# The last step of a spectral branch: block transposes on VectorE replaced by DMAs inside SBUF, and its final matmuls in 64x64 tiles

## The chip, the core and the metric

The kernel runs on one core of one Trainium2 chip. The metric is the device time of one execution in microseconds (us), lower being better. The kernel before takes 149.45 us (median of three runs, 148.86 to 152.55).

## The reference

The kernel computes a gated mix of two branches over the same input x of 2048 positions and 512 channels, in fp32:

```
g = sigmoid((x * gate_w).sum(-1))                # one gate per position
a = irfft2(rfft2(x) * (w_r + 1j * w_i))          # branch A: a 2-D spectral filter
b = irfft(rfft(x, 2L) * rfft(K, 2L))[:L] + x * D_skip   # branch B: a long convolution along positions
out = g * a + (1 - g) * b
```

K is the kernel of a state space model, made from log_A_real, A_imag, C_real, C_imag and log_dt. With the inputs given, every channel of B falls under a test that allows a running sum over positions (a scan) in place of the convolution. A counter of such channels is read at the end; a general path behind it is in the program and isn't taken.

## The kernel before

Branch A is a mixed-radix transform. A position is split as 32 x 64; the kernel works on 32 *slots* (frequencies of the short transform) and handles the slots in nine units: eight pairs and a half one. A hand-written order, the string PLAN, names the work word by word: a letter is a function, a digit its unit. Each word's instructions go to their engines in this order, and each engine runs its own queue in order; all loads, stores and copies that SP issues stand in one queue.

The words, with the lines of the profile of before:

- `f`/`F`, `C`, `c` (L228 to L240): fold the input, first matmuls, a DVE block transpose into AR.
- `P`, `t`, `D`, `d`, `Z`, `z`, `y` (L351 to L390): transform along positions and along channels for one unit, with PE, ACT and DVE taking turns in PSUM.
- `W`, `U` (L403, L405) on DVE, `p`, `g` (L412 to L425) on GpSimd, `h` (L431): the product with the weights w.
- `I`, `i`, `V` (L440 to L453): back along channels; `V` writes the result of a unit into AI, two pieces of 128 x 256 or more for each unit.
- `B`, `e` (L478 to L485): first step back along positions, p_ia, copied from PSUM into AI by ACT. The words `v`, `w`, `j`, `K`, `E`, `H` do the same for one unit in halves of its channels (L496, L499).
- `b` (L503): eight DVE block transposes in place over the whole of AI (seen as VA, 32 columns of 256 channels), which put the slots on the partitions for the last step.
- `Y`, `s` (L511, L516): branch B. PE transposes the scanned x (XT) four columns at a time, ACT scales the result by 1 - g into AR.
- `Q` (L528): the last step of A: for each of 32 columns, one matmul of a 128x128 matrix s1a by VA's 256 columns into p_oa.
- `q` (L549, DVE) or `a`, `A` (L539 on ACT, L543 on GpSimd): g times the result is added to AR, and two stores of 256 KB go out for each group of four columns.

XT is built by `X`, `x`, `m`, `o`, `r`, `k` (L273 to L292): a scan on DVE, and an accumulating DMA (XT<-v, issued by GpSimd) or a DVE instruction (L292) that adds it to the scaled x.

Most intermediate tiles come from one pool, "blk", of 13 blocks; the next tile waits until the oldest one's readers are done. Eight semaphores serve SP's DMAs in turn, so a ninth DMA waits for the first of the eight.

Of the kernel before, what the change touches and what calls it, by code (L numbers as in the profile page):

```python
# [26 lines left out]
ALU = mybir.AluOpType  # L27
# [12 lines left out]
F1 f0 C0 c0 C1 R2 f2 R5 R3 f3 l2 c1 F4 C2 c2 f5 C4 N0 F6 X0 l3 R4 C5 R1 c4 C6 f8 C8 N1 N2 G4 F9 R0 c5 l0 X1 l1 c8 c6  # L40
C9 C3 c9 f7 N3 x0 X2 C7 c3 R6 c7 P1 P0 J0 G5 x1 t1 J1 t0 D1 m0 m1 J2 x2 m2 P2 P4 L2 L1 D0 R9 d1 z1 Z1 y1 t2 D2 t4 W1
U1 L3 d0 z0 p1 Z0 L0 y0 W0 l4 d2 z2 Z2 y2 U0 P6 P5 U2 R8 g1 P3 t5 t6 D5 W2 R7 L4 p0 g0 t3 X3 x3 l5 h1 D3 z3 m3 d3 d5
l7 L5 Z3 z5 y3 h0 W3 U3 l6 p2 I1 i1 V1 G0 P7 g2 Z5 o3 p3 o0 L6 y5 G1 G2 t7 W5 D4 d4 I0 g3 U5 p5 g5 h3 D6 z4 Z4 S3 D7
i0 V0 y4 U4 o1 L7 W4 d7 z6 G3 d6 Z6 h5 l8 y6 z7 r0 P8 p4 t8 B1 W6 Z7 e1 y7 h2 U6 g4 I5 i5 o2 p6 D8 z8 L8 W7 g6 U7 p7
d8 h4 V5 I3 r1 i3 V3 x4 o4 I2 i2 B3 e3 I4 Z8 y8 m4 g7 h6 i4 V2 x6 W8 h7 I6 i6 U8 V6 V4 I7 S2 p8 i7 V7 m6 k6 g8 h8 B2
B6 e6 e2 I8 i8 v8 B5 x7 S1 e5 B4 x5 m7 j8 e4 w8 E8 o5 K8 H8 S0 B7 e7 m5 r2 k7 Y4 Y7 Y1 Y6 b1 s7 s4 Y3 s3 Y0 s0 Y2 Y5
b6 s6 s1 b2 b3 b0 b4 s5 b5 b7 Q6 s2 Q0 q6 q0 Q5 q5 Q3 q3 Q7 Q4 q4 a7 Q2 A7 q2 Q1 q1
# [5 lines left out]
PARTS = [slice(a, b) for a, b in zip([0, 8, 16, 32, 48, 64, 80, 96, 112, 120], [8, 16, 32, 48, 64, 80, 96, 112, 120, 128])]  # L53
CHANNELS = np.concatenate([_T, 256 + _T, 511 - _T, 255 - _T])


def _consts():
# [54 lines left out]
    s2p = s2p.transpose(1, 0, 2)  # L112
# [9 lines left out]
    s1b = np.zeros((32, 2, 2, 32, 32, 2))  # L122
    s1a = np.zeros((32, 2, 2, 16, 2, 2, 32, 2))
    for g in range(2):
        s1b[:, g, :, :, :, g] = s1i[32 * g:32 * g + 32]
        for e in range(2):
            for dh in range(2):
                s1a[:, g, :, :, e, dh, :, g] = s1i[32 * g:32 * g + 32, :, :16] * 2 / 512 * (-1) ** (e * dh)
    s1b = s1b.reshape(32, 128, 64).transpose(1, 0, 2)
    s1a = s1a.reshape(32, 128, 128).transpose(1, 0, 2)  # L130
# [23 lines left out]
def body(ctx: ExitStack, tc: tile.TileContext, x, xg, xt, w, wh, prms, vecs, gw, dskip,  # L154
# [14 lines left out]

    AI = keep.tile([P, 17, D], F32, name="AI")  # L170
    VA = AI[:, 0:16].rearrange("p s (e d) -> p (s e) d", e=2)
# [7 lines left out]
    X = AI.rearrange("p s d -> p (s d)")[:, 0:8192]  # L179

    last = AI[:, 16]
# [11 lines left out]
    gws = work.tile([P, 4, 32], F32, name="gws")  # L193

# [8 lines left out]
    with tc.manual_schedule():  # L203
# [90 lines left out]

        def G_(k):
# [152 lines left out]
        def V_(u, ks=(0, 1)):  # L448
            pr = UNITS[u]
            n = nrow(pr) // 64  # L450
            ai = AI[:, 2 * pr:2 * pr + n].rearrange("p s (h k t) -> p s h k t", h=2, k=2)
            for k in ks:
                V.tensor_tensor(ai[:, :, :, k], t_["pi", u][:, :n, :, 0], t_["po", u][:, :n], op=ALU.subtract if k else ALU.add)  # L453


        def M_(u):
            p = t_["pi", u] = psum("p_v").rearrange("p u (h n) -> p u h n", h=2)
            for v in range(nrow(UNITS[u]) // 64):
                for h in range(2):
                    a = [t_["gt", u][:, o, v, 2 * h:2 * h + 2].rearrange("p c k -> p (c k)") for o in range(2)]  # L460
                    T.matmul(p[:, v, h], a[0], dbw[:, h, 0:1].broadcast_to([P, 2, P]), start=True, stop=False)
                    T.matmul(p[:, v, h], a[1], dbw[:, h, 1:3], start=False, stop=True)

        def o_a(u, ks=slice(0, 2)):
            pr = UNITS[u]
            n = nrow(pr) // 64
            ai = AI[:, 2 * pr:2 * pr + n].rearrange("p s (h k t) -> p s h k t", h=2, k=2)
            pi = t_["pi", u][:, :n].rearrange("p s h (k t) -> p s h k t", k=2)
            S.copy(ai[:, :, :, ks], pi[:, :, :, ks])


        def B_(u):
            pr = UNITS[u]
            p = t_["pb", u] = psum("p_ia")
            for v in range(2):
                sl = 2 * pr + v
                if sl == 0:
                    T.matmul(p[:, v], s2e[:, 0], AI[:, 0], start=True, stop=False)  # L478
                    T.matmul(p[:, v], s2e[:, 16], AI[:, 16], start=False, stop=True)
                else:  # L480
                    T.matmul(p[:, v], s2p, AI[:, sl], start=True, stop=True)  # L481

        def e_a(u):
            pr = UNITS[u]
            S.copy(AI[:, 2 * pr:2 * pr + 2], t_["pb", u])  # L485


        def half(u, k):
            pr = UNITS[u]
            return AI[:, 2 * pr:2 * pr + 2].rearrange("p s (h k t) -> p k s h t", h=2, k=2)[:, k]  # L490

        def B2_(u, k):
            if k == 0:
                t_["pb", u] = psum("p_ia").rearrange("p k (s h t) -> p k s h t", s=2, h=2)
            for v in range(2):
                T.matmul(t_["pb", u][:, k, v], s2p, half(u, k)[:, v], start=True, stop=True)  # L496

        def e2_a(u, k):
            S.copy(half(u, k), t_["pb", u][:, k])  # L499

        def b_a(c):
            v = VA[:, :, 32 * c:32 * c + 32].rearrange("p b d -> p d b")
            V.transpose(v, v)  # L503


        def Y_(j):
            p = t_["py", j] = psum("p_y").rearrange("p k (b i d) -> p (k b) i d", b=2, i=2)
            xv = XT.rearrange("p (i e) (c b) -> p i (e c) b", i=2, b=32)
            for k in range(4):
                for i in range(2):  # L510
                    T.transpose(p[:, k, i], xv[:, i, :, 4 * j + k], eye)  # L511

        def s_a(j):
            for k in range(4):
                b = 4 * j + k
                S.activation(AR[:, b].rearrange("p (i d) -> p i d", i=2), t_["py", j][:, k], AF.Copy, scale=g1[:, 1, b:b + 1])  # L516
# [4 lines left out]
        def load_a(k):  # L521
            s1a[k] = work.tile([P, 8, P], F32, tag="w", name="s1a", bufs=4)
            nc.sync.dma_start(s1a[k], c_s1a[:, 8 * k:8 * k + 8])

        def Q_(j):
            p = t_["pq", j] = psum("p_oa").rearrange("p k (b d) -> p (k b) d", b=2)
            for k in range(4):
                T.matmul(p[:, k], s1a[j // 2][:, 4 * j % 8 + k], VA[:, 4 * j + k], start=True, stop=True)  # L528
# [6 lines left out]
        def a_a(j):  # L535
            t_["qs", j] = blk([P, 4, 256], "qs")
            for k in range(4):
                b = 4 * j + k
# [7 lines left out]
        def q_a(j):  # L546
            for k in range(4):
                b = 4 * j + k
                V.scalar_tensor_tensor(AR[:, b], t_["pq", j][:, k], g1[:, 0, b:b + 1], AR[:, b], op0=ALU.mult, op1=ALU.add)  # L549
# [19 lines left out]
            "v": lambda u: V_(u, (0,)), "w": lambda u: V_(u, (1,)), "j": lambda u: B2_(u, 0), "K": lambda u: B2_(u, 1), "E": lambda u: e2_a(u, 0), "H": lambda u: e2_a(u, 1),  # L569
# [225 lines left out]
```

## Time and profile before

| | us |
|---|---|
| median of three runs | 149.45 (148.86 to 152.55) |
| the profiled execution | 148.65 |
| its span | 146.8 |
| TensorE's mean granted clock in it | 0.95 of full speed |
| PE busy | 112.6 |
| DVE busy | 113.8 |
| ACT busy | 70.5 |
| GpSimd busy | 57.4 |

The profile is of one execution. The span reaches from its first to its last instruction, and the execution's time lies 1.85 us above it. PE is TensorE's matmuls, PEld its weight loads, DVE is VectorE, ACT ScalarE, POOL GpSimd, SP the engine that issues most DMAs; SPq is SP's queue. L503 is line 503 of the kernel. In a group of instructions, "out<-in" names the tiles, then come the shape, the count, the time busy, the mean of one in ns, and after the bar the time that the engine idled just before them with what ended it. An fp32 matmul is recorded as two instructions of half the work each, so 32 matmuls are 64 records.

### The profile page before, as it was taken

The page shows a single profiled execution, that of the slowest core. Times are in us where ns is not written, and L with a number is a line of the kernel's source. Part 1 is how long each engine was busy: PE and PEld are TensorE (multiplying, and loading weights), DVE is VectorE, ACT ScalarE, POOL GpSimd, SP SyncE. Part 2 cuts the span into 40 slices and gives each one's busy share as a digit, 9 for nine tenths or more (in the row PEclk, how much of TensorE's full clock was granted, in tenths as well). Part 3 has the DMA queues.
Part 4 walks back from the last instruction along what each step waited for, and adds up shares of the span by engine and source line. Part 5 has one row for each costly group of instructions (what it writes and reads, how often), then busy time and mean ns, then how long its engine had stood idle before and what let it go on. Part 6 is the DMA issues. An engine that isn't in the chain of part 4 may idle for free.

```text
span 146.8 us, 1834 instructions
## 1 busy us (share of the span) xinstructions
PE 112.6 (77%) x611; PEld 86.1 (59%) x611; DVE 113.8 (78%) x134; ACT 70.5 (48%) x136; POOL 57.4 (39%) x57
## 2 busy tenths in 40 slices
PE   7936976399989998959888878997805975999600
PEld 7811352098978982858378577462405964888400
DVE  0369999995788597759798995979689997695900
ACT  0003000337375969496789765398610699504000
POOL 0306850100059993976999979200200000003300
PEclk9999999959999999999999999999975899999985
DMA  4999999992105870404793898000191000158690
GB/s 114 318 275 418 391 417 387 413 416 99 37 7 173 287 292 0 143 5 146 132 225 91 273 214 210 4 0 0 40 214 36 0 0 0 57 205 318 223 354 19
DMA packets 9427, 25.52 MB, mean 174 GB/s; under 512 B 1568, under 2 KB 2624, under 8 KB 8512
## 3 DMA queue, kind: packets, MB, share of 16 engines
q1 hardware_dynamic: 8976, 22.16, 42.2%
q0 software_dynamic: 432, 3.15, 10.9%
q8 instruction: 7, 0.11, 0.3%
q14 instruction: 12, 0.10, 0.2%
HBM read 17.93 MB, written 4.19 MB: 151 GB/s over the span
## 4 chain that ended last, share of the span: by engine, by line
DVE 31%; PE 30%; ACT 17%; DMA 9%; issue 5%; POOL 2%; SPq 1%; DVEq 0%; ACTq 0%; POOLq 0%
DVE AR L240 9%; PE p_oa L528 8%; PE p_d L365 6%; ACT AR L516 6%; PE p_t L351 5%; DMA XT<-v 5%; PE p_v L440 5%; DMA AI<-in_x_dram 5%; DVE v L283 3%; DVE p_d L378 3%; DVE p_d L379 3%; DVE tw L405 3%; PE p_ia L481 2%; PE p_y L511 2%; DVE AR L549 2%
## 5 line engine op out<-in xcount | busy, mean ns | idle before, releaser
L351 PEld LDWEIGHTS p_t<-s2e,AR 128*128 128x128 f32 x136 | 17.4, 208 | 5.5 <-DVE AR L240 3.5
L351 PE MATMUL p_t<-s2e,AR 128*128 128x128 f32 x136 | 18.0, 294 | 3.4 <-DVE AR L240 2.7
L440 PEld LDWEIGHTS p_v<-dbw,gt 128*128 128x128 f32 x136 | 16.0, 192 | 7.5 <-issue 4.6
L440 PE MATMUL p_v<-dbw,gt 128*128 128x128 f32 x136 | 16.8, 278 | 4.6 <-ACT gs L303 1.5
L236 PE MATMUL p_s<-f,AI 128*128 128x512 f32 (+1 forms) x40 | 15.7, 527 | 5.5 <-DVE f L228 3.4
L412 POOL TENSOR_TENSOR px<-tw 128x512 f32<-128x512 f32 (+1 forms) x9 | 10.9, 1215 | 19.6 <-DVE tw L405 19.5
L503 DVE STREAM_TRANSPOSE AI<-AI 128x1024 f32<-128x1024 f32 x8 | 16.9, 2202 | 1.8 <-ACT AI L485 1.8
L365 PE MATMUL p_d<-et,dfw 128*128 128x256 f32 (+1 forms) x72 | 16.1, 371 | 0.7 <-ACT et L356 0.6
L240 DVE STREAM_TRANSPOSE AR<-p_s 128x1024 f32<-128x1024 f32 (+1 forms) x10 | 14.8, 1555 | 1.6 <-PE p_s L236 1.6
L516 ACT ACTIVATE AR<-p_y,g 128x256 f32<-128x256 f32 x32 | 11.8, 587 | 8.1 <-PE p_y L511 8.1
L528 PE MATMUL p_oa<-AI,s1a 128*128 128x256 f32 x64 | 14.1, 380 | 1.7 <-ACT AR L516 1.7
L511 PE MATMUL p_y<-eye,XT 128*128 128x128 f32 x64 | 10.0, 317 | 6.5 <-DMA XT<-v 5.6
L277 ACT ACTIVATE p_x<-XT,pers 128x1024 f32<-128x1024 f32 x8 | 9.0, 1121 | 12.5 <-POOL pers L261 10.4
L549 DVE SCALAR_TENSOR_TENSOR AR<-p_oa,g,AR 128x256 f32<-128x256 f32 x28 | 11.6, 477 | 4.2 <-PE p_oa L528 4.0
L236 PEld LDWEIGHTS p_s<-f,AI 128*128 128x128 f32 x40 | 7.1, 196 | 13.1 <-issue 4.3
L365 PEld LDWEIGHTS p_d<-et,dfw 128*128 128x128 f32 x72 | 12.7, 190 | 2.5 <-ACT et L356 1.2
L528 PEld LDWEIGHTS p_oa<-AI,s1a 128*128 128x128 f32 x64 | 12.1, 190 | 3.5 <-ACT AR L516 1.9
L543 POOL TENSOR_TENSOR AR<-AR,qs 128x1024 f32<-128x1024 f32 x1 | 2.3, 2348 | 29.2 <-ACT qs L539 29.2
L511 PEld LDWEIGHTS p_y<-eye,XT 128*128 128x128 f32 x64 | 9.2, 201 | 7.8 <-issue 6.3
L453 DVE TENSOR_TENSOR AI<-p_v,po 128x512 f32<-128x512 f32 (+1 forms) x18 | 10.9, 650 | 2.3 <-ACT po L445 2.3
L405 DVE TENSOR_TENSOR tw<-p_d,w 128x1024 f32<-128x1024 f32 x8 | 9.8, 1219 | 3.6 <-ACT p_d L390 3.6
L481 PE MATMUL p_ia<-AI,s2p 128*128 128x512 f32 x26 | 12.0, 595 | 0.0
(66 smaller groups left out, 180.6 us busy)
## 6 DMA issues: line engine op xcount, KB each, us to landing
w<-in_w_dram SPq DMA_DIRECT2D x8, 512.0 KB, 5.6
XT<-in_xt_dram SPq DMA_DIRECT2D x4, 1024.0 KB, 7.0
out_dram<-AR SPq DMA_DIRECT2D x16, 256.0 KB, 3.7
AI<-in_x_dram SPq DMA_DIRECT2D x6, 512.0 KB, 7.6
XT<-v POOLq DMA_DIRECT2D x3, 1024.0 KB, 7.0
s1a<-in_c_s1a_dram SPq DMA_DIRECT2D x4, 512.0 KB, 3.9
AI<-in_x_dram SPq DMA_DIRECT2D x4, 256.0 KB
prm<-in_prms_dram SPq DMA_DIRECT2D x3, 256.0 KB
```

The costliest lines, as they stand in the source:

```text
L236: T.matmul(p[:, u, :n], s1e, t_["f", q][:, u, :n], start=True, stop=True)
L240: V.transpose(AR.rearrange("p s (u d) -> p u d s", u=2)[:, :, PARTS[q]], t_["c", q][:, :, :32 * n].rearrange("p u (b d) -> p u d b", d=n))
L351: T.matmul(p[:, q, :, 64 * v:64 * v + 64], AR[:, 16 * (q // 2) + sl, 128 * (q % 2):128 * (q % 2) + 128], s2e[:, k], start=True, stop=True)
L365: T.matmul(p[:, o, :, h, :n], dfw[:, 2 * h + o], et[:, ::-1] if h else et, start=True, stop=True)
L405: E.tensor_tensor(t.rearrange("p o r a k -> p (o r a k)"), z.rearrange("p o q k -> p (o q k)"), w.rearrange("p o r a k -> p (o r a k)"), o ...
L440: T.matmul(p[:, v, h, o], t_["gt", u][:, o, v, 2 * h:2 * h + 2].rearrange("p c k -> p (c k)"), dbw[:, h, o], start=True, stop=True)
L481: T.matmul(p[:, v], s2p, AI[:, sl], start=True, stop=True)
L503: V.transpose(v, v)
L511: T.transpose(p[:, k, i], xv[:, i, :, 4 * j + k], eye)
L516: S.activation(AR[:, b].rearrange("p (i d) -> p i d", i=2), t_["py", j][:, k], AF.Copy, scale=g1[:, 1, b:b + 1])
L528: T.matmul(p[:, k], s1a[j // 2][:, 4 * j % 8 + k], VA[:, 4 * j + k], start=True, stop=True)
L549: V.scalar_tensor_tensor(AR[:, b], t_["pq", j][:, k], g1[:, 0, b:b + 1], AR[:, b], op0=ALU.mult, op1=ALU.add)
```

## The change

1. The eight DVE block transposes are gone. Word `b` now belongs to a unit: ACT copies p_ia into a block tile ei, and four DMAs on SP's queue (one for each slot and half of the channels) write it into VA so that the slots come to lie on the partitions. Each of the 32 DMAs reads 128 partitions of 1 KB and writes 4 partitions, 32 apart, of 32 KB. AI is gone; the input X, which shared its space, now shares VA's. `V` writes into a block tile ai, and the halves (`v`, `w`, `j`, `K`, `E`, `H`) are gone.
2. The last step `Q` is done in 64x64 tiles: for each column two matmuls, one for each half of VA's partitions, at the array's four quadrants in turn: columns k = 0 and 1 of a group of four on the diagonal, 2 and 3 on the other two. s1a holds 64 columns in place of 128 for each position.
3. The output's rows come in another order (g, half, a), so B's part must match: `s` scales into a block tile sc, and a new word `w` moves it into AR with four DMAs of 128 KB (32 partitions of 4 KB to 32 partitions). The gates go through a tile gh, and eight DMAs of 4 KB put them in the same order. The host puts the rows back.
4. PLAN is a new order. The copies `e` and DMAs `b` of the first pairs stand in the middle of the kernel; part of `Y` and `s` stands ahead of the last pairs; all of `Q` is at the end.

The general path, which isn't taken, is changed to match. The core of the diff:

```diff
-    AI = keep.tile([P, 17, D], F32, name="AI")
-    VA = AI[:, 0:16].rearrange("p s (e d) -> p (s e) d", e=2)
+    VA = keep.tile([P, 32, 256], F32, name="VA")
...
+LAST = np.array([2 * j + k % 2 + 16 * (k // 2) for j in range(8) for k in range(4)])
...
+        def regroup(dst, src):
+            for g in range(2):
+                for e in range(2):
+                    nc.sync.dma_start(dst[64 * g + 32 * e:64 * g + 32 * e + 32], src[64 * e + g:64 * e + 64:2])
...
         def V_(u, ks=(0, 1)):
             pr = UNITS[u]
             n = nrow(pr) // 64
-            ai = AI[:, 2 * pr:2 * pr + n].rearrange("p s (h k t) -> p s h k t", h=2, k=2)
+            if 0 in ks:
+                t_["ai", pr] = blk([P, 2, D], "ai")
+            ai = t_["ai", pr][:, :n].rearrange("p s (h k t) -> p s h k t", h=2, k=2)
...
         def e_a(u):
-            pr = UNITS[u]
-            S.copy(AI[:, 2 * pr:2 * pr + 2], t_["pb", u])
+            t_["ei", u] = blk([P, 2, D], "ei")
+            S.copy(t_["ei", u], t_["pb", u])
...
-        def b_a(c):
-            v = VA[:, :, 32 * c:32 * c + 32].rearrange("p b d -> p d b")
-            V.transpose(v, v)
+        def b_a(u):
+            for v in range(2):
+                for e in range(2):
+                    nc.sync.dma_start(VA[4 * UNITS[u] + 2 * v + e::32], t_["ei", u][:, v, 256 * e:256 * e + 256])
...
         def s_a(j):
+            t = t_["sc", j] = blk([P, 4, 2, P], "sc")
             for k in range(4):
-                b = 4 * j + k
-                S.activation(AR[:, b].rearrange("p (i d) -> p i d", i=2), t_["py", j][:, k], AF.Copy, scale=g1[:, 1, b:b + 1])
+                b = LAST[4 * j + k]
+                S.activation(t[:, k], t_["py", j][:, k], AF.Copy, scale=gh[:, b:b + 1])
+
+        def r_a(j):
+            regroup(AR[:, 4 * j:4 * j + 4].rearrange("p k d -> p (k d)"), t_["sc", j].rearrange("p k i d -> p (k i d)"))
...
         def load_a(k):
-            s1a[k] = work.tile([P, 8, P], F32, tag="w", name="s1a", bufs=4)
-            nc.sync.dma_start(s1a[k], c_s1a[:, 8 * k:8 * k + 8])
+            s1a[k] = work.tile([P, 16, 64], F32, tag="w", name="s1a", bufs=4)
+            nc.sync.dma_start(s1a[k], c_s1a[:, 16 * k:16 * k + 16])
 
         def Q_(j):
             p = t_["pq", j] = psum("p_oa").rearrange("p k (b d) -> p (k b) d", b=2)
-            for k in range(4):
-                T.matmul(p[:, k], s1a[j // 2][:, 4 * j % 8 + k], VA[:, 4 * j + k], start=True, stop=True)
+            for k in (0, 2, 1, 3):
+                for r in (0, 64):
+                    o = r ^ 64 * (k // 2)
+                    T.matmul(p[o:o + 64, k], s1a[j // 4][r:r + 64, 4 * (j % 4) + k], VA[r:r + 64, LAST[4 * j + k]], start=True, stop=True, tile_position=(r, o))
```

The end of the new order, from the first inner DMAs on (b5, b1, b7, b3, b8, b2, b4, b6 for the eight pairs; w is the move of a scaled group):

```
... U3 W3 I2 d4 L4 r0 I0 g8 i2 t6 i0 B5 p3 Z4 h8 V0 I1 V2 y4 U4 e5 b5 x4 B2 W4 I8 o3 g7
h7 m4 e2 i1 V1 r1 i8 V8 x5 D6 I7 m5 z6 g3 o4 B1 o5 i7 l6 h3 V7 d6 Z6 x6 e1 L6 p4 m6 I3 i3 r2 k6 B8 e8 x7 V3 B7 b1 m7
k7 y6 e7 B3 e3 b7 b3 Y6 Y2 b8 W6 s6 w6 g4 h4 Y5 s5 Y0 s0 I4 Y1 U6 p6 g6 h6 S1 i4 V4 w0 s1 I6 i6 w5 s2 B4 b2 V6 w1 e4
b4 B6 e6 Y4 s4 Y3 s3 b6 w2 Y7 w4 Q1 Q6 w3 s7 w7 q1 Q7 a7 q6 Q5 q5 Q4 q4 A7 Q2 Q0 q2 Q3 q0 q3
```

More of the change, by code (lines that the diff above doesn't have):

```diff
@@ L178, in body @@
     XT = work.tile([P, 4, L], F32, name="XT")
-    X = AI.rearrange("p s d -> p (s d)")[:, 0:8192]
-    last = AI[:, 16]
+    X = VA.rearrange("p s d -> p (s d)")
+    last = work.tile([P, 388], F32, name="last")
     s1e, ones = last[:, 0:128], last[:, 128:256]
@@ L193, in body @@
     gws = work.tile([P, 4, 32], F32, name="gws")
+    gh = work.tile([P, 32], F32, name="gh")
     def blk(shape, name):
@@ L547, in q_a @@
             for k in range(4):
-                b = 4 * j + k
-                V.scalar_tensor_tensor(AR[:, b], t_["pq", j][:, k], g1[:, 0, b:b + 1], AR[:, b], op0=ALU.mult, op1=ALU.add)
+                b, o = LAST[4 * j + k], 4 * j + k
+                V.scalar_tensor_tensor(AR[:, o], t_["pq", j][:, k], g1[:, 0, b:b + 1], AR[:, o], op0=ALU.mult, op1=ALU.add)
             store(j)
```

106 lines of the change are left out of this document (46 added, 60 removed).

## The prediction, made before the changed kernel had run

> **What bounds the kernel now.** I read the page first, for the shares; then the table by stages; then the timeline and the chain of the last third, which is the part that the change rebuilds.
>
> ```profile
> span 146.8 us, 1834 instructions
> ...
> PE 112.6 (77%) x611; PEld 86.1 (59%) x611; DVE 113.8 (78%) x134; ACT 70.5 (48%) x136; POOL 57.4 (39%) x57
> ...
> DVE 31%; PE 30%; ACT 17%; DMA 9%; issue 5%; POOL 2%; SPq 1%; DVEq 0%; ACTq 0%; POOLq 0%
> ```
>
> No engine fills the span: DVE and PE are busy for three quarters of it and share the chain, so the answer lies in stages.
>
> ```profile
> 0.00:60.00 60.00, 49.30 (x273) 36.26 (x274) 46.66 (x56) 22.07 (x39) 24.94 (x31) 0.97 0.69 249
> 60.00:80.00 20.00, 17.11 (x100) 13.76 (x99) 16.14 (x21) 15.95 (x34) 17.61 (x15) 1.00 0.50 129
> 80.00:90.00 10.00, 7.74 (x54) 6.33 (x54) 8.32 (x10) 7.88 (x14) 8.92 (x8) 1.00 0.90 217
> 107.00:124.00 17.00, 9.75 (x63) 8.97 (x63) 16.91 (x8) 8.86 (x26) 0.00 (x0) 0.80 0.23 46
> 124.00:139.80 15.80, 14.05 (x64) 12.08 (x64) 11.60 (x28) 4.50 (x13) 2.35 (x1) 1.00 0.54 195
> 139.80:146.80 7.00, 0.00 (x0) 0.00 (x0) 0.01 (x1) 0.00 (x0) 0.00 (x0) 0.68 0.48 177
> ```
>
> The columns after the stretch are PE, PEld, DVE, ACT, POOL, clock, DMA share, GB/s. From 107 to 124 us DVE is full with eight instructions; from 124 to 139.8 PE is full; the last 7.0 us are the stores' landing and the end of the program. The timeline says what those stages are:
>
> ```profile
> 107.05 16.91 DVE L503 STREAM_TRANSPOSE AI<-AI 128x1024 f32<-128x1024 f32 x8 [1.84 <-ACT AI L485]
> 115.15 11.78 ACT L516 ACTIVATE AR<-p_y,g 128x256 f32<-128x256 f32 x32 [8.14 <-PE p_y L511]
> 124.06 14.05 PE L528 MATMUL p_oa<-AI,s1a 128*128 128x256 f32 x64 [1.75 <-ACT AR L516]
> 126.13 6.77 DVE L549 SCALAR_TENSOR_TENSOR AR<-p_oa,g,AR 128x256 f32<-128x256 f32 x16 [2.17 <-PE p_oa L528]
> 134.70 5.11 DVE L549 SCALAR_TENSOR_TENSOR AR<-p_oa,g,AR 128x256 f32<-128x256 f32 x12 [1.79 <-PE p_oa L528]
> ```
> ```profile
> 104.58 6.97 DMA XT<-v
> ...
> 115.15 8.87 ACT AR L516 x24
> ...
> 124.06 12.34 PE p_oa L528 x56
> ```
>
> The last stage's matmuls (L528) start at 124.06, when two chains meet: the eight transposes (107.05 + 16.91 = 123.96), and the chain's own way over the late XT DMA and ACT's scaled copies (115.15 + 8.87 = 124.02). So the transposes are only half of the wait: take them away alone and the ACT path still ends at 124. The reordering has to move both.
>
> **The change, part by part.** Removed: 16.9 us of DVE transposes. Every word of the last stage needs all eight pairs of slots, so its start is the landing of the last inner DMA.
>
> (1) *Inner DMAs.* For each pair, four DMAs of 128 KB: source 128 partitions of 1 KB, target four partitions (32 apart) of 32 KB. How many DMA engines does such a shape use? The trace has a small one with an outer dimension of four at its source, the gate's scatter (8 KB in 64 pieces of 128 B), and the stores for comparison:
>
> ```profile
> DMA packets 68, 0.01 MB, mean 16 GB/s; under 512 B 68, under 2 KB 68, under 8 KB 68
> ...
> g<-gs SPq DMA_DIRECT2D x1, 8.0 KB
> ```
> ```profile
> DMA packets 2316, 4.32 MB, mean 216 GB/s; under 512 B 256, under 2 KB 256, under 8 KB 2304
> ...
> q1 hardware_dynamic: 2304, 4.20, 57.1%
> ...
> out_dram<-AR SPq DMA_DIRECT2D x16, 256.0 KB, 3.7
> ```
>
> Sixteen stores of 128 rows are 2048 data packets; the other 256 are small: 16 for each store, one for each engine it ran on. The scatter has 64 data packets and 4 small ones: four engines. So I take it that each inner DMA runs on four engines, 32 KB on each. [...]
>
> The price of a KB on one engine, from both sides. Stores: 57.1% of 16 engines in 20 us is 183 us for 2048 packets of 2 KB, 44 ns per KB. The one large transfer from SBUF to SBUF:
>
> ```profile
> q0 software_dynamic: 144, 1.05, 64.9%
> ...
> XT<-v POOLq DMA_DIRECT2D x1, 1024.0 KB, 7.0
> ```
>
> 64.9% of 16 engines in 8 us is 83 us for 128 packets of 8 KB: 81 ns per KB. It accumulates (two reads), so it is an upper bound; but it is the row nearest in kind, with both ends in SBUF, and the inner DMAs' small pieces and few target rows are no help to them. I take 72, three quarters of the way up. Then one inner DMA takes 32 x 72 = 2.3 us, a pair 9.2, all eight 73.7 (45 at 44; 83 at 81). [...]
>
> (2) *When this stream can begin.* DVE's work ahead of the final stage, without the transposes, is 113.8 - 16.9 - 11.6 = 85.3 us.
>
> ```profile
> L453 DVE TENSOR_TENSOR AI<-p_v,po 128x512 f32<-128x512 f32 x16 | 10.1, 680 | 2.3 <-ACT po L445 2.3
> ...
> L405 DVE TENSOR_TENSOR tw<-p_d,w 128x1024 f32<-128x1024 f32 x8 | 9.8, 1219 | 3.6 <-ACT p_d L390 3.6
> ...
> L283 DVE TENSOR_TENSOR_SCAN v<-pers,v,p_x 128x1024 f32<-128x1024 f32 x4 | 9.4, 2344 | 2.1 <-ACT p_x L277 2.0
> ...
> L379 DVE TENSOR_TENSOR p_d<-ds,p_d 128x512 f32<-128x512 f32 x8 | 5.6, 696 | 0.3
> ...
> L378 DVE TENSOR_TENSOR p_d<-p_d,ds 128x512 f32<-128x512 f32 x8 | 5.5, 691 | 1.7 <-ACT first L384 1.7
> ...
> L292 DVE SCALAR_TENSOR_TENSOR XT<-XT,pers,v 128x1024 f32<-128x1024 f32 x2 | 2.5, 1272 | 0.0
> ```
>
> In the new order, DVE still has behind the first finished pair (V5) seven full V words (14 x 0.68), a half one (0.8), six products (1.22), two Z (1.39), four scans (2.3) and two L292 (1.27): 32 us. So V5 ends after 53 us of DVE work. The kernel before has done 46.7 by 60 us and 62.8 by 80, so that is at 68; with matmul and copy 71 to 74. The first copy of the kernel before agrees:
>
> ```profile
> L485 ACT COPY AI<-p_ia x7: 998/1012/1018, 74.0 to 106.0; 128x1024 f32<-128x1024 f32 x7
> ```
>
> I take 73. The next inner word (b1) needs V1, which has 20 us of DVE work behind it: work 65.3, at 83, with matmul and copy 86. The others (b7, b3, b8) follow faster than 9 us apart.
>
> (3) *What shares those four engines.* From 73 on, ahead of the last inner DMA in SP's order: four of the eight regroup words (each four DMAs of 128 KB with 32 rows on both sides; 32 KB on every engine, 1.4 us at 44 ns), 5.6; a weight load and an s1a load, 2.8; two XT DMAs, 64 KB x 81 = 5.2 each, 10.4. Sum with the inner DMAs: 92.5 us. The stream never runs dry (b5, a load and an XT DMA fill 73 to 89), so the last inner DMA ends at 165.5. It lands 1 us later, half of what a whole 128 KB load takes from issue to landing:
>
> ```profile
> s2e<-in_c_s2p_dram SPq DMA_DIRECT2D x1, 128.0 KB, 2.1
> ...
> L342 SPq DMA_DIRECT2D w<-hT x9: 573/597/760, 35.0 to 78.9; - x9
> ```
>
> SP's issues (0.6 each for the shape on four engines, above) come to some 19 us for all 32 and hide under the 92. SP runs in order: behind a regroup that waits for its sc copy stand the next inner DMAs, and behind all of them the sixteen stores; the stores are late anyway. Buffers: of the 13 blocks, s4 waits for b1's DMAs, s7 for b7's and the px of the last unit for b5's, all landed long before 165. The eight scaled copies (11.8 us of ACT) move ahead of the last pairs, into time in which ACT waits. They cost nothing while the inner stream covers them.
>
> (4) *Last stage in 64x64 tiles.* 64 matmuls of half the rows and half the columns in place of 32.
>
> ```profile
> L300 PE MATMUL p_gate<-XT,gws 128*32 128x512 f32 x32 | 3.6, 595 | 0.0
> ```
>
> Here 32 records of 595 ns, on four column tiles, take 3.6 us, so four run at a time in fp32. Four at a time, 128 records at 14.05/64 = 0.22 us come to 7.0 us; serial they would be 28.1. PE's 14.05 falls under DVE's 28 instructions, 6.77 + 5.11 = 11.9 us, which then set the tail: 0.9 for the first word and 11.9. That saves 139.8 - 124.06 - 12.8 = 3 us. The four regroups behind the last inner DMA (5.6) land ahead of the DVE words that read them, the first three of which need older ones.
>
> (5) *Rest.* The gate gets eight 4 KB DMAs in the middle, the transposes read columns in LAST's order, s1a halves its columns but not its bytes: nothing on the path.
>
> Sum: 165.5 + 1 + 12.8 + 7.0 = 186.3 of span. The profiled execution took 148.65 with a span of 146.8, so add 1.85: 188.2. The median of the runs (149.45) lies 0.8 above that execution: 189.
>
> **Rivals.** *A: the same four engines, at the stores' price.* At 44 ns a pair takes 5.6 us, the stream waits for b1 at 86, and then has seven pairs 39.4, regroups 5.6, a load 1.4, one XT 5.2: ends at 137.6; the same tail gives 161. For it: the stores' row. Against it: no store reads 1 KB pieces or writes to four rows. *B: the inner DMAs are hidden.* Were they spread over 16 engines, a pair would take 1.4 us, and the last stage would begin after the last V: 107 as before, 3 for matmul and copy, 2.4 for four issues, 2.1 to land, 114.5; then 12.8, 7.0 and 2.65: 137, faster by 8%. This decides once a pair takes under 4.0 us, (127 - 1 - 86 - 12.2)/7, with 127 the start that makes no difference; that is 31 ns per KB on four engines, under the cheapest row, so it needs more engines. Against it stand the 68 packets. *C: the tiles run serially* (the change doesn't do what it says): 28.1 in place of 12.8 behind the same stream, 205. Against it stands the gate row.
>
> **How the numbers follow.** Forecast 0.60, A 0.25, B 0.10, C 0.05. The forecast's own range is 175 to 203 (81 ns for inner DMAs and regroups: 14 us more). The range reaches down to A without the XT transfer in its stream, 156, and leaves out B and C. Faster by over 2% (about what a measurement can tell here): 0.10, B. Within 2%: 0.03, between A and B. Slower: 0.87.
>
> **What would show it.** PE idle before the last stage with a DMA on VA as its releaser; the last-stage matmuls starting near 166; DMA share near a quarter (four of 16) in the stretch before it, some 60 GB/s; the inner DMAs' packets 1 KB with 4 small ones each; L543 on DVE 28 in one run of 12 us; last-stage records over about 7 us of work. I am wrong if the start of the last stage is under 130 (B), if ACT or PE rather than a DMA releases it, or if the inner DMAs land within 3 us of issue while several are in flight.

## The result, and the profile after

The changed kernel takes 221.3 us (median of four runs, 220.4 to 223.1), the kernel before 149.7 on the same chip: 1.483 times as long, 95% interval 1.468 to 1.498. The prediction was 189, 156 to 203: slower as forecast, but 18 us past the upper end. Ratios with an interval are of a kernel's undisturbed executions, those within 1.5% of its fastest.

The page of the changed kernel: the span, the busy slices of PE, the granted clock, DMA and GB/s (40 slices of 5.5 us each), SP's queue, two groups of the last stage, and the transfer that adds the scan to XT:

```profile
span 221.1 us, 2064 instructions
PE   8858759899999889725899000000000000009400
PEclk9976999999999999995899955555555555557965
DMA  6999942733370949951222222874672227438993
GB/s 203 301 406 399 408 188 58 326 95 93 111 275 24 189 78 161 184 115 38 59 49 51 49 49 47 123 107 110 131 108 46 62 49 112 74 72 177 316 370 140
q1 hardware_dynamic: 14832, 29.54, 49.6%
L543 DVE SCALAR_TENSOR_TENSOR AR<-p_oa,g,AR 128x256 f32<-128x256 f32 x28 | 11.2, 475 | 83.3 <-DMA AR<-sc 83.2
L522 PE MATMUL p_oa<-VA,s1a 64*64 64x256 f32 x128 | 8.8, 437 | 76.4 <-DMA AR<-sc 76.4
XT<-v POOLq DMA_DIRECT2D x3, 1024.0 KB, 15.2
```

PE's row is empty from the 23rd to the 36th slice. In six of these 14 slices DMA stands at 2 tenths and the rate at 46 to 62 GB/s; in the other eight more goes on, as the regroup words' DMAs run too. The windows say the same by stretch (start:end and length, then busy us and count of each engine, the granted clock, the DMA share, GB/s):

```profile
73.00:104.00 31.00, 22.40 (x105) 14.57 (x106) 22.42 (x24) 19.62 (x31) 15.06 (x13) 0.93 0.73 128
104.00:130.00 26.00, 16.79 (x106) 12.95 (x104) 6.13 (x7) 17.25 (x41) 5.05 (x4) 0.89 0.28 50
130.00:198.00 68.00, 0.00 (x0) 0.00 (x0) 0.00 (x0) 0.00 (x0) 0.00 (x0) 0.50 0.51 85
198.00:221.00 23.00, 8.76 (x128) 5.87 (x128) 11.19 (x28) 1.57 (x4) 2.34 (x1) 0.72 0.78 245
```

For 68 us no engine computes anything. What goes on is in SP's own timeline (start, length, queue, line, transfer, count), where L490 are the inner DMAs, L303 the regroup words, L526 the stores; below it the two rows of the last stage from the timeline of PE and DVE:

```profile
77.50 2.33 SPq L490 DMA_DIRECT2D VA<-ei  x4
80.27 0.33 SPq L351 DMA_DIRECT2D w<-in_w_dram  x1
103.17 0.66 SPq L356 DMA_DIRECT2D w<-hT  x1
103.93 31.53 SPq L490 DMA_DIRECT2D VA<-ei  x16
135.57 5.12 SPq L303 DMA_DIRECT2D AR<-sc  x4
142.09 0.34 SPq L515 DMA_DIRECT2D s1a<-in_c_s1a_dram  x1
147.00 10.22 SPq L303 DMA_DIRECT2D AR<-sc  x8
157.46 2.52 SPq L490 DMA_DIRECT2D VA<-ei  x4
160.08 2.75 SPq L303 DMA_DIRECT2D AR<-sc  x4
163.47 18.44 SPq L490 DMA_DIRECT2D VA<-ei  x8
181.96 22.71 SPq L303 DMA_DIRECT2D AR<-sc  x16
204.77 10.80 SPq L526 DMA_DIRECT2D out_dram<-AR  x16
198.49 8.76 PE L522 MATMUL p_oa<-VA,s1a 64*64 64x256 f32 x128 [76.38 <-DMA AR<-sc]
200.53 11.26 DVE L543 SCALAR_TENSOR_TENSOR AR<-p_oa,g,AR 128x256 f32<-128x256 f32 x28 [83.22 <-DMA AR<-sc]
```

The inner stream begins at 77.5, stands between 80 and 103 behind one small row of weights (w<-hT), and the last stage starts at 198.5. PE's operands are VA and s1a; that its row names AR<-sc as releaser, not VA<-ei, is the profile's inference, for SP's DMAs share eight semaphores (141 issues on eight in this trace).

The price of one inner DMA is read where only they run, in the DMA view of 110 to 130 us:

```profile
q1 hardware_dynamic: 998, 0.99, 28.8%
```

28.8% of 16 engines' 20 us is 92 us, over 968 packets of 1 KB (and 30 small ones): 95 ns each. The 30 small ones are four for each 128 of 1 KB, one for each engine by the prediction's reading; the share is 4.6 engines' work, so on four the records of an engine overlap, and what a KB costs is read from the rate: 0.99 MB in 20 us is 50 GB/s, a DMA of 128 KB (0.131 MB) takes 2.65 us, and a KB on one of four engines 83 ns.

### The profile page after: what moved, and what is told of

It reads as the page before. It is cut to its first block, busy times and chain, and to the rows that moved or that the text cites. A ratio compares the mean times of both kernels' runs of the same rounds, so it can differ in the third digit from the quotient of the medians.

```text
span 221.1 us, 2064 instructions
## 1 busy us (share of the span) xinstructions
PE 109.1 (49%) x671; PEld 78.0 (35%) x671; DVE 99.6 (45%) x126; ACT 70.6 (32%) x135; POOL 57.4 (26%) x57
## 5 line engine op out<-in xcount | busy, mean ns | idle before, releaser
L522 PE MATMUL p_oa<-VA,s1a 64*64 64x256 f32 x128 | 8.8, 437 | 76.4 <-DMA AR<-sc 76.4
L522 PEld LDWEIGHTS p_oa<-VA,s1a 64*64 64x64 f32 x128 | 5.9, 157 | 79.0 <-issue 77.5
L533 ACT ACTIVATE qs<-p_oa,g 128x256 f32<-128x256 f32 x4 | 1.6, 474 | 73.2 <-PE p_oa L522 73.2
L241 PE MATMUL p_s<-f,last 128*128 128x512 f32 (+1 forms) x40 | 18.8, 613 | 5.5 <-DVE f L233 5.0
L480 PE MATMUL p_ia<-ai,s2p 128*128 128x512 f32 x30 | 16.3, 666 | 7.7 <-DVE ai L469 6.2
L379 PE MATMUL p_d<-et,dfw 128*128 128x256 f32 (+1 forms) x72 | 16.3, 374 | 1.7 <-DVE v L288 0.6
L469 DVE TENSOR_TENSOR ai<-p_v,po 128x512 f32<-128x512 f32 (+1 forms) x18 | 10.8, 653 | 7.7 <-ACT po L459 6.2
L504 ACT ACTIVATE sc<-p_y,gh 128x256 f32<-128x256 f32 x32 | 12.3, 476 | 5.5 <-DMA VA<-ei 4.8
L241 PEld LDWEIGHTS p_s<-f,last 128*128 128x128 f32 x40 | 8.4, 226 | 15.2 <-issue 10.2
L288 DVE TENSOR_TENSOR_SCAN v<-pers,p_x 128x1024 f32<-128x1024 f32 x4 | 9.1, 2275 | 7.0 <-DMA XT<-v 7.0
L438 POOL TENSOR_TENSOR gt<-px 128x512 f32<-128x512 f32 (+1 forms) x9 | 11.4, 1272 | 2.8 <-PE p_v L454 2.4
L439 POOL TENSOR_TENSOR gt<-px 128x512 f32<-128x512 f32 (+1 forms) x9 | 11.4, 1269 | 0.0
## 6 DMA issues: line engine op xcount, KB each, us to landing
XT<-v POOLq DMA_DIRECT2D x3, 1024.0 KB, 15.2
```

Source lines behind the costliest of these rows:

```text
L241: T.matmul(p[:, u, :n], s1e, t_["f", q][:, u, :n], start=True, stop=True)
L379: T.matmul(p[:, o, :, h, :n], dfw[:, 2 * h + o], et[:, ::-1] if h else et, start=True, stop=True)
L438: G.tensor_tensor(gv[:, :, 0], src[0], src[1], op=ALU.add)
L439: G.tensor_tensor(gv[:, ::-1, 1], src[0], src[1], op=ALU.subtract)
L480: T.matmul(p[:, v], s2p, t_["ai", pr][:, v], start=True, stop=True)
L504: S.activation(t[:, k], t_["py", j][:, k], AF.Copy, scale=gh[:, b:b + 1])
```

## The experiments

The four runs of the changed kernel lie within 2.7 us; most kernels here were run once, so differences under 3 us are not read. "Last stage" is the start of the run of matmuls into p_oa that does most of it (in x_tiles, of the first run).

| kernel | edit | last stage at | us |
|---|---|---|---|
| changed kernel | | 198.5 | 221.3 |
| x_ports | inner targets 4 rows apart, not 32 | 156.0 | 181.4 |
| x_4k | inner sources 32 rows of 4 KB | 188.9 | 213.8 |
| x_adjacent | inner targets side by side | 203.2 | 228.3 |
| x_rows | inner DMAs over 128 rows | 120.3 | 151.6 |
| x_regroup | regroup words over 128 rows | 190.3 | 215.5 |
| x_regdst / x_regsrc / x_regboth | regroup targets / sources / both spread | 187.1 / 199.6 / 192.2 | 211.7 / 224.0 / 216.7 |
| x_ports_regroup | x_ports and x_regroup | 150.0 | 174.6 |
| x_noacc | no accumulating DMAs | 183.4 | 208.3 |
| x_b5late | first inner DMAs behind L6 | 192.4 | 217.0 |
| x_rows_regroup | x_rows and x_regroup | 119.5 | 152.8 |
| x_rows_store | and the stores on ACT's queue | 123.4 | 155.4 |
| x_tiles | the kernel before, last stage alone in 64x64 tiles | 128.5 | 150.4 |

### Where the four engines write: x_ports, x_4k, x_adjacent

```diff
-nc.sync.dma_start(VA[4 * UNITS[u] + 2 * v + e::32], t_["ei", u][:, v, 256 * e:256 * e + 256])
+nc.sync.dma_start(VA[16 * UNITS[u] + 2 * v + e:16 * UNITS[u] + 16:4], t_["ei", u][:, v, 256 * e:256 * e + 256])
```

> The changed kernel with the inner DMAs aimed at four rows that lie 4 apart (16u + 2v + e, and 4, 8 and 12 further) in place of 32 apart; sources, bytes and pieces stay, the rows of VA and so the output are other ones. Theory 1, two of the four engines share a way into the target because rows 32 apart lie behind one port: a 1 KB piece falls from 95 ns to about 50, a DMA from 2.7 to 1.5 us, 28 of them give back some 33 us, the last stage starts near 165 in place of 198.5 and the time is about 187 us. Theory 2, a 1 KB piece between two on-chip buffers costs 95 ns on its engine wherever it goes: start within 3 us of 198.5, time 218 to 224 us.

It took 181.4 us, 40 less: theory 1, and 6 us better than it said. The DMA view of x_ports from 98 to 108 us, inner DMAs alone again, and below it the last stage in its timeline:

```profile
q1 hardware_dynamic: 962, 0.95, 27.1%
```

```profile
156.00 8.78 PE L522 MATMUL p_oa<-VA,s1a 64*64 64x256 f32 x126 [7.69 <-DMA VA<-ei]
```

About as many packets as above in half the time, at nearly the same share of busy engines: 27.1% of 160 us over 932 of 1 KB (30 are small) is 46.5 ns, and 0.95 MB in 10 us is 95 GB/s. The small packets (four for each 128 of 1 KB again), the bytes, the pieces and the sources are the same; only the rows of the target moved. Here PE's releaser is VA<-ei, as it should be.

x_4k tells whether the price hangs on the piece:

```diff
-nc.sync.dma_start(VA[4 * UNITS[u] + 2 * v + e::32], t_["ei", u][:, v, 256 * e:256 * e + 256])
+nc.sync.dma_start(VA[4 * UNITS[u] + 2 * v + e::32].rearrange("p s d -> p (s d)").rearrange("p (r x) -> p r x", x=1024), t_["ei", u][64 * v + 32 * e:64 * v + 32 * e + 32].rearrange("p v d -> p (v d)"))
```

> The changed kernel with each inner DMA reading 32 rows of 4 KB in place of 128 rows of 1 KB; the same four target rows and the same 128 KB on four engines, so the output is another one. Theory 2a, each piece has a fixed cost of about 50 ns beside 44 ns per KB (the price of the stores): a 4 KB piece takes some 230 ns, a DMA 1.8 us in place of 2.7, 28 of them give back 25 us, start near 173, time near 196 us. Theory 2b, an engine moves bytes between two on-chip buffers at about 95 ns per KB whatever the piece: a 4 KB piece takes about 380 ns and the time stays at 218 to 224 us.

213.8 us, and from 106 to 116 us:

```profile
q1 hardware_dynamic: 148, 0.54, 25.8%
```

Without 16 small packets that is 132 of 4 KB at 313 ns, 78 per KB: below theory 2b's 95, far above theory 2a's 58. The time, too, lies between the two and nearer to 2b. So the price goes mainly by bytes. Larger pieces, which here also come from 32 rows in place of 128, raise the rate from 50 to 54 GB/s (132 x 4 KB in 10 us) and bring 7.5 us; other targets nearly double it and bring 40 us.

x_adjacent goes the other way, with the four rows side by side:

```diff
+nc.sync.dma_start(VA[16 * UNITS[u] + 8 * v + 4 * e:16 * UNITS[u] + 8 * v + 4 * e + 4], t_["ei", u][:, v, 256 * e:256 * e + 256])
```

> The changed kernel with the four target rows of each inner DMA side by side (in place of 32 apart); bytes, pieces and sources stay, the rows of VA and so the output are other ones. x_ports, with rows 4 apart, brought the 1 KB piece from 95 to 46 ns and the time from 221.3 to 181.4 us. Theory 1, groups of four neighbouring rows lie behind one way in, and rows 32 apart share it too: now four engines write through one, a piece takes about 185 ns, a DMA 5.5 to 6 us, and the step from 46 to 95 ns (40 us) is paid twice more: 295 to 312 us. Theory 2, only rows 32 apart hinder one another: a piece stays near 46 ns and the time near 181 us.

228.3 us: neither. The GB/s rows (40 slices) of two windows of the DMA view tell more, 112 to 118 us first and 130 to 140 us below:

```profile
GB/s 55 27 20 41 102 184 96 55 27 27 27 27 27 27 27 27 27 27 27 27 27 27 14 21 21 27 27 27 27 27 27 41 41 68 48 20 20 20 27 27
```

```profile
GB/s 66 74 66 74 74 74 66 74 74 86 86 74 74 70 78 74 74 66 82 90 82 49 57 70 74 66 57 90 86 45 37 53 45 74 78 66 74 78 41 45
```

In most slices of the first window the stream runs at 27 GB/s, half of the changed kernel's 50 and a quarter of what x_ports reached, about as theory 1 says. Later it runs at some 74. The three rates, 27, 50 and 95, stand nearly as 1, 2 and 4. Theory 1 reads them so: rows share ways into the memory, four neighbouring rows one, the changed kernel's four rows two, those of x_ports four. The rates agree; the ways themselves are in no record. A reading of the 74 is argued and not shown either, for the records carry no engine: in x_adjacent the next DMA of a pair writes to a different group of four rows, so an engine that has got ahead would find another way in free. In the changed kernel all four DMAs of a pair write into rows 4u to 4u+3 and those 32, 64 and 96 further, by this reading the same ways in, and getting ahead by one DMA would help nothing.

x_4k's 54 GB/s, with the changed kernel's target rows, lies beside its 50, and the 95 of x_ports is about what four engines move at the stores' 44 ns per KB (93, an estimate).

### Sixteen engines: x_rows

```diff
+nc.sync.dma_start(VA[:, 4 * UNITS[u] + 2 * v + e], t_["ei", u][:, v, 256 * e:256 * e + 256])
```

> The changed kernel with each inner DMA as a copy from 128 rows to the same 128 rows, 1 KB each; the same bytes and number of pieces, spread over 16 engines, and VA gets no transpose, so the output is another one. Theory 1, the four engines set the price: 8 pieces on each engine in place of 32, at 95 ns 0.8 us a DMA, 28 of them give back 53 us of the stream; what is left is the last V at 117 to 119 with its copies and the regroup words at 2.5 to 4 us each, so the last stage starts between 135 and 150 and the time is 157 to 172 us. Rival, all copies inside the core share one limit near 49 GB/s, however many engines: start near 198, time 218 to 224 us.

151.6 us, 70 less and below what theory 1 expected: with this one term spread over 16 engines (16 small packets for each DMA: 128 beside 1032 of 1 KB from 92 to 100 us) the kernel is about as fast as before. DVE's group then waits for the regroup words:

```profile
L543 DVE SCALAR_TENSOR_TENSOR AR<-p_oa,g,AR 128x256 f32<-128x256 f32 x28 | 11.3, 477 | 18.3 <-DMA AR<-sc 16.8 <-PE p_oa L522 1.6
```

### The regroup words: x_regroup, x_regdst, x_regsrc, x_regboth, x_ports_regroup

```diff
-nc.sync.dma_start(dst[64 * g + 32 * e:64 * g + 32 * e + 32], src[64 * e + g:64 * e + 64:2])
+x_regroup: for k in range(4): nc.sync.dma_start(AR[:, 4 * j + k], t_["sc", j][:, k].rearrange("p i d -> p (i d)"))
+x_regdst:  nc.sync.dma_start(dst[2 * g + e:P:4], src[64 * e + g:64 * e + 64:2])
+x_regsrc:  nc.sync.dma_start(dst[64 * g + 32 * e:64 * g + 32 * e + 32], src[2 * e + g:P:4])
+x_regboth: nc.sync.dma_start(dst[2 * g + e:P:4], src[2 * e + g:P:4])
```

> The changed kernel with each of the eight regroup words as four copies of 128 rows by 1 KB in place of four of 32 rows by 4 KB; inner DMAs as they are, the same bytes, AR gets its rows unordered, so the output is another one. Theory 1, copies of 32 rows on both sides are slow as such (300 to 470 ns per 4 KB piece): a word falls to about 1.4 us, some 12 us come back, start near 187, time near 209 us. Theory 2, a copy between on-chip buffers costs some 95 ns per KB on its engine whatever the rows: 32 pieces of 95 ns, 3 us a word, start 195 to 199, time 216 to 223 us.

> The changed kernel with every regroup copy aimed at 32 rows that lie 4 apart over all 128 rows, in place of 32 neighbouring rows; its source, 32 rows 2 apart in one half, and its 4 KB pieces stay. Rows land elsewhere (the gate's regroup too), so the output is another one. Theory 1, a regroup piece took 300 ns in place of 159 because 16 engines write into 32 neighbouring rows, which lie behind half of the ways in: pieces fall to 159 to 200 ns outside the inner stream, time 213 to 217 us as for x_regroup. Theory 2, reading from 64 rows of one half is what is slow: pieces stay near 300 ns, time 219 to 223 us.

> The changed kernel with every regroup copy reading 32 rows that lie 4 apart over all 128 rows, in place of 32 rows 2 apart in one half; its target, 32 neighbouring rows, and its 4 KB pieces stay. Other rows are copied (the gate's too), so the output is another one. Theory 1 (target): pieces stay near 300 ns, time 219 to 223 us. Theory 2 (source): pieces fall to 159 to 200 ns outside the inner stream, time 213 to 217 us.

> The changed kernel with every regroup copy reading 32 rows that lie 4 apart and writing 32 rows that lie 4 apart, both over all 128 rows; 4 KB pieces as before. Other rows are copied and land elsewhere (the gate's too), so the output is another one. Theory 1, the two sides have a cost each: pieces fall to 159 to 170 ns in the stretch without inner DMAs and the time falls at least as far as with the targets alone, 207 to 212 us. Theory 2, the 10 us of x_regdst did not come from the regroup words: 216 to 223 us.

The times were 215.5, 211.7, 224.0 and 216.7. The DMA view of 5 us in which only these words run (SP's queue: packets, MB, share), in the changed kernel from 199 on:

```profile
q1 hardware_dynamic: 298, 0.84, 77.7%
```

x_regdst from 188 on:

```profile
q1 hardware_dynamic: 296, 0.82, 72.8%
```

x_regsrc from 200.5 on:

```profile
q1 hardware_dynamic: 288, 0.78, 55.6%
```

and x_regboth from 193 on, with the issues in it:

```profile
q1 hardware_dynamic: 302, 0.84, 43.1%
AR<-sc SPq DMA_DIRECT2D x7, 128.0 KB
```

With the 92 to 98 small packets taken out of the count, a 4 KB piece took 300, 290, 235 and 170 ns. So both sides count: the lowest price, 170, came with sources and targets over all rows. The times fit no pair of theories as a whole. x_regroup lies just under theory 2's range. In x_regdst the pieces stayed near 300, as theory 2 says, and yet the time fell below theory 1's range. x_regsrc has theory 1's time, 1 us over, with pieces between the theories, and x_regboth theory 1's pieces with theory 2's time.

Yet 0.78 to 0.84 MB are moved in 5 us in all four views, for SP hands out seven DMAs in that time, one in 0.7 us, whatever a piece costs (the row of issues is the same in all four). And part of the differences arose ahead of the first copy: b5 was issued at 77.5 in the changed kernel, at 75.1, 74.8, 78.3 and 78.4 in the four runs. From the first of these copies in SP's timeline to the last stage the changed kernel needs 62.9 us, x_regroup 58.8, x_regdst 57.0, x_regsrc 63.2 and x_regboth 58.3. So cheaper pieces are worth some 4 to 6 us, and 6.0 beside the mended inner DMAs (42.2 in x_ports, 36.3 here):

> x_ports (inner targets 4 rows apart) and x_regroup (regroup words as copies of 128 rows by 1 KB) together; the same bytes, rows unordered, so the output is another one. Theory 1, the regroup pieces at 300 ns per 4 KB, on 16 engines, still hold up the inner stream and the tail in x_ports: 168 to 176 us. Theory 2, SP's order and the issues hold it (about 1.2 us an inner DMA in x_ports): 178 to 182 us.

174.6 us against 181.4: theory 1. Why other targets alone give as much as both sides, and other sources alone nothing, stays open.

### The start of the stream: x_noacc, x_b5late

```diff
-            G.dma_start(XT[:, k], t_["v", k].rearrange("p h l -> p (h l)"), accum_op=ALU.add)
+            pass
```

> The changed kernel without the three accumulating DMAs that add the scans to XT on 16 engines, so the output lacks those sums. In the changed kernel b5's DMAs (issued at 77.5) and the weight load l6 share the engines with them, the row w<-hT waits for l6 until 103, and the rest of the inner stream is issued behind it. Theory 1, this sharing made the stream start late: w<-hT goes by 86, b1's DMAs by 92, the last stage starts 9 to 12 us earlier than 198.5 and the time is 208 to 213 us. Theory 2, the start is set by the work on DVE and ACT ahead of b1, or the stream loses elsewhere what it gains: 217 to 222 us.

> The changed kernel with one word moved: b5, the first full pair's inner DMAs, behind L6 in place of ahead of l6. The result is the same. Theory 1, SP's in-order wait is what costs (28.1 us at L356, of which l6 behind b5 makes most): L6 goes near 85, b5 and b1 follow at once, last stage 5 to 10 us earlier, time 211 to 216 us. Theory 2, the four engines work without a gap from 77.5 on either way, so that moving a word only changes the order of the same work: within 3 us of 221.

x_noacc took 208.3 us, 13 less, at the good end of theory 1. From SP's and PE's timelines of x_noacc:

```profile
91.43 0.66 SPq L356 DMA_DIRECT2D w<-hT  x1
92.19 30.70 SPq L490 DMA_DIRECT2D VA<-ei  x16
183.39 8.66 PE L522 MATMUL p_oa<-VA,s1a 64*64 64x256 f32 x128 [69.94 <-DMA AR<-sc]
```

and of x_b5late, which keeps the transfers and only issues b5 later:

```profile
79.04 0.62 SPq L349 DMA_DIRECT2D w<-hT  x1
79.77 51.06 SPq L483 DMA_DIRECT2D VA<-ei  x20
192.38 8.57 PE L515 MATMUL p_oa<-VA,s1a 64*64 64x256 f32 x128 [71.00 <-DMA AR<-sc]
```

217.0 us, between the theories. There w<-hT passes 24 us sooner and the last stage comes 6 sooner. Most of SP's wait in the changed kernel, from 80.6 to 103.2, was therefore no loss: engines were at work meanwhile. The DMA view of the changed kernel from 76 to 106 us (40 slices) has them at 9 tenths from 82 to 95.5 and then at 2 tenths, some four engines' work, until 102:

```profile
DMA  9101223899999999999999999953222222210002
```

What cost time is the work itself, and x_noacc shows it for the sums into XT.

### What all 16 engines leave: x_rows_regroup, x_rows_store

> The changed kernel with the inner DMAs as copies of 128 rows (as in x_rows) and the regroup words as copies of 128 rows too (as in x_regroup); bytes stay, neither reorders its rows, so the output is another one. It is the prediction's rival B measured: all 16 engines on every word. x_rows took 151.6 us, with L543 waiting 16.8 us for AR<-sc. Theory 1, these regroup pieces (300 ns per 4 KB in place of 159) were the last hold of x_rows: they land 2 to 4 us each sooner and the time is B's, 135 to 141 us. Theory 2, what holds x_rows is SP's order: sixteen stores (11.7 us for 4 MB) stand behind 28 inner and 32 regroup DMAs of 0.6 us an issue, and start no earlier than 130: 146 to 150 us.

```diff
-                nc.sync.dma_start(out[:, j, k:k + 2], AR[:, 4 * j + k:4 * j + k + 2])
+                nc.scalar.dma_start(out[:, j, k:k + 2], AR[:, 4 * j + k:4 * j + k + 2])
```

> x_rows_regroup (all 16 engines on the inner DMAs and the regroup words, rows unordered, so the output is another one) with the sixteen stores issued by ACT in place of SP. There SP issues the last sixteen regroup copies until 135 us and only then the stores, 10.8 us of them. Theory 1, SP's order is what keeps rival B's 137 away: the stores of the first finished groups leave from 119 on, only the last ones wait for the last regroup word, and the time falls from 152.8 to 143 to 148 us. Theory 2, the stores' 4 MB or DVE's words set the end whatever queue issues them: 151 to 154 us.

152.8 and 155.4 us, both above either theory's range, so rival B's 137 isn't reached even with all 16 engines on every copy. The timelines of x_rows_regroup:

```profile
103.83 2.48 SPq L509 DMA_DIRECT2D AR<-sc  x4
...
123.12 11.79 SPq L509 DMA_DIRECT2D AR<-sc  x16
135.00 10.82 SPq L527 DMA_DIRECT2D out_dram<-AR  x16
129.85 5.97 DVE L544 SCALAR_TENSOR_TENSOR AR<-p_oa,g,AR 128x256 f32<-128x256 f32 x15 [0.60 <-DMA AR<-sc]
```

and of x_rows_store:

```profile
126.49 12.64 SPq L509 DMA_DIRECT2D AR<-sc  x16
129.57 19.33 ACTq L527 DMA_DIRECT2D out_dram<-AR  x14
```

From 104 to 135 SP issues 44 inner and regroup DMAs and one load without a gap, 0.6 to 0.75 us each, while the DMA engines are 62% busy (SP's queue from 112 to 122), and DVE's last words wait for the last of them. Taking the stores off SP changed little: from the last regroup copy issued to the end of the span are 16.0 us in the one and 14.4 in the other, and x_rows_store had everything 4 us later. So theory 1 of x_rows_store falls. That the issuing of the inner and regroup DMAs sets this end is read from the rows; no run took it away.

### The last stage alone: x_tiles

The line that puts the rows in order; the matmuls of `Q` are those of the changed kernel:

```diff
+for g in range(2):   # rows put in order (g, e, a) where PE turns XT
+    T.matmul(p[64 * g:64 * g + 64, k, i], xv[:, i, g, :, LAST[4 * j + k]], eye, start=True, stop=True, tile_position=(0, 64 * g))
```

> The kernel before with one part of the change alone: the last stage in 64x64 tiles, four at a time, and rows (g, half, a). The transposes stay on DVE as in the kernel before, no inner and no regroup DMAs; the rows are put in order where PE transposes XT, with two products of 64 columns in place of one of 128. The result is the same. Theory 1 (step 4 of the prediction): PE's 14 us fall to 7 to 9, DVE's 28 words of 11.9 us set the tail, 3 us less: 145 to 148 us. Theory 2, the two half products run one after the other and add up to 10 us of PE work ahead of the last stage, or the stores set the tail anyway (4 MB, 11 us): 149 to 155 us.

150.4 us (median of 12), 1.009 times the kernel before (95% interval 1.0044 to 1.0135): theory 2. The windows of x_tiles, and three rows of its timelines:

```profile
112.00:128.50 16.50, 16.29 (x254) 16.16 (x255) 13.54 (x6) 8.24 (x23) 0.00 (x0) 0.88 0.01 2
128.50:141.00 12.50, 7.86 (x130) 4.48 (x128) 11.06 (x28) 5.32 (x15) 2.34 (x1) 0.95 0.60 213
```

```profile
128.49 2.00 PE L538 MATMUL p_oa<-AI,s1a 64*64 64x256 f32 x32
129.72 11.06 DVE L559 SCALAR_TENSOR_TENSOR AR<-p_oa,g,AR 128x256 f32<-128x256 f32 x28 [4.18 <-ACT AR L524]
130.62 14.72 SPq L542 DMA_DIRECT2D out_dram<-AR  x16
```

and the kernel before in the stretch ahead of its last stage:

```profile
107.50:124.00 16.50, 9.75 (x63) 8.97 (x63) 16.46 (x8) 8.85 (x25) 0.00 (x0) 0.79 0.20 40
```

From the first last-stage matmul to DVE's end went from 15.7 us (124.06 to 139.8) to 12.3 (128.49 to 140.8): 3.4 saved, as step 4 had it. But little of this reaches the end of the span: from DVE's end to there are 9.6 us (150.4 - 140.8) in place of 7.0, as SP issues the sixteen stores until 145.3, in the kernel before until 141.0. Counted from the first matmul to the end of the span 21.9 us stand against 22.7, 0.8 saved. And the half products take PE 16.3 us in place of 9.8 ahead of the stage, which starts 4.4 later. The profiled execution of x_tiles is the longest of its twelve, 152.2 us, so up to 2 us of these differences may be its own.

## Why the prediction was wrong, step by step

The span of 221.1 is 34.8 above the sum's 186.3. (The median's error, 32.3, is smaller because the profiled execution, 223.1, is 1.8 above the median.)

- *Step 1, the inner DMAs.* Four engines, 32 KB on each, 1 KB packets, a quarter of DMA's share (28.8%): all as said. That all 32 DMAs have the same four engines, on which the sum rests, no run shows, as the records carry no engine; what they show is that while SP issued an inner DMA every 2.7 us (six in 16.1 us from 116.8 on), the share stayed at 28.8% and the rate at 50 GB/s. The term was mis-sized: 72 ns per KB was taken from between two rows of other transfers, and 83 was measured by the rate. For the 28 DMAs behind b5 that is 74.2 us (28 x 2.65) against 64.4: +9.8. The upper of the two rows, 81, would have been near, but by luck, as it is of a transfer over all rows on 16 engines (16 small packets beside 128) that also accumulates. The choice between the rows was blind to what sets the price, which x_ports and x_adjacent show: where the four target rows lie (95 GB/s with rows 4 apart, 50 with 32, 27 with the rows side by side).
- *Step 2, when the stream starts.* 77.5 in place of 73: +4.5; the first pair was ready that much later.
- *Step 3, what shares the engines.* The step that failed most, and the one that carries the time out of the range, whose upper end already had 81 ns per KB for inner DMAs and regroup words. b5, the weight load and two XT transfers were put at 21.0 us (9.2, 1.4 and 10.4); from 77.5 to b1's first DMA at 103.9 were 26.4: +5.4. The two XT<-v issued at 79.9 and 87.8 took 17.0 and 15.2 us to land in place of 7 (the one issued at 70.3, ahead of the stream, 7.3). Without all three the last stage came 15.1 us sooner, with b5 issued 1.3 sooner. What is left up to the last stage, 121.0 - 26.4 - 74.2 = 20.4 us for four regroup words, a load and the landing, had been put at 8.0: +12.4. Two parts of it can be named. A regroup word was costed at 44 ns per KB, the price of stores from all rows, on all 16 engines, 1.4 us. Sixteen engines are near what its view shows (92 small packets beside 206 of 4 KB, 14 for each DMA of 32; 77.7% busy). But its pieces took 300 ns per 4 KB, as sources and targets each lie in part of the rows (170 in x_regboth, with both over all rows): 2.4 us a word (an estimate, 32 KB at 75 ns), 4 us more for four, and x_regroup and x_regboth gave 4.1 and 4.6 back between the first copy and the last stage. And "the stream never runs dry" did not hold. The DMA view of 152 to 158 us, and from the waits of SP's queue those for inner DMAs ahead of regroup copies (us in total, times, the longest):

```profile
DMA packets 301, 0.86 MB, mean 143 GB/s; under 512 B 91, under 2 KB 91, under 8 KB 301
SPq L303 <- DMA VA<-ei: 19.5, 7, 4.5
```

  In these 6 us not one packet is a 1 KB inner piece: 91 are under 512 B, the other 210 are over 2 KB. SP was issuing the eight regroup copies that begin at 147.0, after waits for earlier inner DMAs whose semaphores they share, and b2's DMAs stand behind them, issued at 157.5, though ACT had made their copy by 81 (the second at L484, at 80.1). The prediction saw that inner DMAs stand behind regroup words in SP's order, and gave it no time. That SP's order makes this gap is read from the rows; no run moved b2. What the remaining 2 us are is not shown.
- *Step 4, the tiles.* Nearly four at a time: 8.8 us of PE against 7.0 (with the granted clock at half when they begin, 0.50 from 130 to 198), far from the 28.1 of rival C. The saving of 3 us is x_tiles' 3.4 up to DVE's end, of which 0.8 was left at the end of the span there.
- *Step 5, the end.* DVE's words began 2.0 us behind PE's and took 11.3, 0.5 over the 12.8. From their end to the end of the span went 9.3 us in place of 7.0: the sixteen stores couldn't leave before SP had issued the last regroup copy at 204.7, and then needed 10.8. Together +2.8. The prediction had seen the stores behind them and called them late anyway.

4.5 + 5.4 + 9.8 + 12.4 + 2.8 = 34.9.

Of the signs named, PE's idle time, the DMA share (28%), the rate (50 GB/s for 60), the packets and DVE's single run came as written; the start of the last stage (198.5 for 166) and its releaser's name did not. *Rival A* is x_ports: the stores' price was nearly reached, 46.5 ns, yet the time was 181 and not 161, as step 3's other terms were too low there as well. *Rival B* is x_rows_regroup: hidden, as it says, but 152.8 and not 137, since the regroup words and SP's issues, which the sum had behind other work, are on its path.

## What to carry to other kernels

Before a transfer inside the chip replaces an engine's transpose, ask how many engines serve it and, for both of its sides, where its rows lie: here four target rows gave 27, 50 or 95 GB/s, side by side, 32 apart or 4 apart. A rate borrowed from a transfer over all 128 rows, 44 ns per KB, held neither for four rows (83, 32 apart) nor for 32 (75). Count what else stands in the same queue, and in which order: here the inner stream stood dry for 6 us behind copies that are only read in the last stage, and with 16 engines on everything 44 DMAs and a load at 0.6 to 0.75 us an issue filled the 31 us ahead of the stores. And a faster last stage is worth only what the stores behind it and the reordering ahead of it leave over: x_tiles won 3.4 us up to DVE's end, 0.8 up to the end of the span, and paid 4.4.

## What the runs showed of the hardware that was not expected

- Four engines writing 1 KB pieces reach 95 GB/s with target rows 4 apart and 50 with rows 32 apart; with rows side by side the stream falls to 27 GB/s, and later in the same run, with DMAs to different groups of rows following each other, it stands at some 74.
- Copies of 32 rows on 16 engines took 300 ns per 4 KB as written and 170 with both sides spread over all rows; spreading only the targets (290) or only the sources (235) gets part of the way at most.
- An accumulating transfer of 1 MB on GpSimd's queue took 17.0 and 15.2 us to land beside the inner DMAs, 7.3 ahead of them and 7.0 in the kernel before; without the three such transfers the last stage came 15.1 us sooner (x_noacc).
